# Full-attention layers: exponentials of one key tile on VectorE instead of ScalarE

## The chip, the cores and the metric

The kernel runs on one core of a Trainium2 chip. Its time is the device time of one execution in microseconds: 2757.82 us, the median of 3 runs (2757.58 to 2761.83).

## What is computed

Four attention layers in turn over a sequence of 2048 rows of 512 values: layer norm, projection to queries, keys and values (32 heads of 16), attention, output projection, addition to the input. Layers 0 and 2 see a window of 256 keys, layers 1 and 3 all 2048. Cut to the full layer:

```python
qkv = (layernorm(x) @ wqkv).reshape(B, S, 3, 32, 16)
scores = einsum("bhqd,bhkd->bhqk", q, k) * 16 ** -0.5
p = softmax(scores)
x = x + einsum("bhqk,bhkd->bhqd", p, v).reshape(B, S, 512) @ wo
```

## The kernel before, in words

**Tiles.** The queries are cut into 4 chunks of 512 rows (`c`), the heads into 8 quads of 4 (`qd`), the keys into 16 tiles of 128 (`j`). In a full layer `attn_full` (L763) walks a quad's 16 key tiles. A tile has two halves `pr` of two heads. For each half `exps` issues 8 score matmuls on TensorE (L727, rows `s<-qt,kt`) into one of two PSUM tiles `s` of 128x1024, and one exponential on ScalarE (L735, `e<-s`), so a quad has 32 of them. The values of a key tile (L779, `acc<-e,vt`) are 8 matmuls that add into the two banks `acc`. They are not issued at once but put into `pvq`, and `flush` issues them a tile later, in front of the next tile's second half. A column of ones in `vt` gives the softmax's denominator.

**The end of a quad.** Behind its last values `epilogue` (L683) adds the two `acc` banks on VectorE into `sa` (L415 and L416) and transposes it into `ot`; the next quad's first values need these banks again. The division by the denominator and, for every second quad, the transpose and split into two fp16 parts `oh` (L709 to L712, the low part on GpSimd) follow from a queue.

**Side work.** All else of the layer and much of the next one is cut into `Work` objects: projections (`project`, `values`), the output projection (`wo`, `wo_part`), layer norm, and checks of the weights' range (`verify`). `Side.share` puts some of their matmuls between the key tiles. In a full layer they use one side bank of two PSUM banks, `PH["halves"]` (rows `b`), which VectorE reads out (`join`, L415 and L416 with `j` or `vt`; L653 and L677 with `x`) before the next use.

**What sets the order.** In the full layers the order on TensorE and VectorE is written by the program itself with a planner's clock: every matmul adds an estimate to `clock`, a key tile takes at least 1.8. VectorE's work that can wait goes into four queues `VQ` (`soon`); `drain` issues it when the estimate `vt_` of VectorE's backlog is less than 0.2 ahead of `clock`. Both engines then work in exactly that order, each waiting where data isn't ready. ScalarE takes the exponentials in the order of their scores. In the windowed layers only TensorE's order is fixed in this way, and a step's exponentials go through GpSimd's masks before the values (L812).

## Time and profile before

| | us |
|---|---|
| median of 3 runs | 2757.82 |
| profiled execution | 2759.5 |
| its span | 2757.7 |
| prologue and layer 0 (0 to 495.2) | 495.2 |
| layer 1, full (495.2 to 1447.0) | 951.8 |
| layer 2, windowed (1447.0 to 1783.6) | 336.6 |
| layer 3, full (1783.6 to 2737.8) | 954.2 |
| tail | 19.9 |

In rows of the profile PE is TensorE, DVE is VectorE, ACT is ScalarE, POOL is GpSimd. A group's row has the line, the engine, the operation, output and input tiles with their shapes, the count, then the busy time in us, the mean duration of one in ns, and the idle time before them with what ended it. A row of the timeline has the start, the time to the end, and the same names. A row of waits has who waited for whom, the total in us, how often, and the longest.

### The profile page before, as it was taken

The page shows a single profiled execution, that of the slowest core. Times are in us where ns is not written, and L with a number is a line of the kernel's source. Part 1 is how long each engine was busy: PE and PEld are TensorE (multiplying, and loading weights), DVE is VectorE, ACT ScalarE, POOL GpSimd, SP SyncE. Part 2 cuts the span into 40 slices and gives each one's busy share as a digit, 9 for nine tenths or more (in the row PEclk, how much of TensorE's full clock was granted, in tenths as well). Part 3 has the DMA queues.
Part 4 walks back from the last instruction along what each step waited for, and adds up shares of the span by engine and source line. Part 5 has one row for each costly group of instructions (what it writes and reads, how often), then busy time and mean ns, then how long its engine had stood idle before and what let it go on. Part 6 is the DMA issues. An engine that isn't in the chain of part 4 may idle for free.

```text
span 2757.7 us, 112292 instructions
## 1 busy us (share of the span) xinstructions
PE 2496.1 (91%) x50513; PEld 1100.3 (40%) x50513; DVE 1094.9 (40%) x2314; ACT 2362.9 (86%) x2683; POOL 515.8 (19%) x1074
## 2 busy tenths in 40 slices
PE   7888989999989999999998898899899999998987
PEld 3233334444433344444443333534444444433332
DVE  5564554122343335325326566323333333333333
ACT  4556654899999999999995667399999999999997
POOL 1445552001000000100105678100000000000000
PEclk9999999999999999999999999999999999999999
DMA  8888856322342224324225565623232333333332
GB/s 286 226 241 240 244 178 191 96 83 82 100 120 79 86 93 137 102 78 126 93 73 169 157 181 143 175 72 109 84 107 90 98 97 104 112 104 123 114 120 103
DMA packets 335035, 359.67 MB, mean 130 GB/s; under 512 B 113616, under 2 KB 250320, under 8 KB 328144
## 3 DMA queue, kind: packets, MB, share of 16 engines
q1 hardware_dynamic: 334544, 352.40, 42.3%
q8 instruction: 397, 6.50, 1.0%
q14 instruction: 94, 0.77, 0.1%
HBM read 239.60 MB, written 96.99 MB: 122 GB/s over the span
## 4 chain that ended last, share of the span: by engine, by line
ACT 56%; PE 23%; issue 11%; DVE 5%; DMA 3%; POOL 2%; SPq 0%; ACTq 0%; DVEq 0%; POOLq 0%
ACT e L735 55%; PE b L402 10%; PE acc L812 3%; PE acc L779 3%; PE bs L402 2%; PE s L731 2%; PE s L727 2%; PE b L399 1%; POOL e L802 1%; POOL e L805 1%; DMA qt<-qs 1%; DMA kt<-kw 0%; DMA wr<-in_A_wo_dram 0%; DVE ot L694 0%; DMA w<-wd 0%
## 5 line engine op out<-in xcount | busy, mean ns | idle before, releaser
L735 ACT ACTIVATE e<-s 128x1024 f32<-128x1024 f32 (+2 forms) x2432 | 2238.8, 1058 | 121.0 <-PE s L731 95.3
L779 PE MATMUL acc<-e,vt 64*17 64x512 f32 x16384 | 1085.0, 590 | 1.3 <-issue 1.3
L727 PE MATMUL s<-qt,kt 64*32 64x512 f16 x16384 | 849.0, 380 | 130.4 <-ACT e L735 106.6
L727 PEld LDWEIGHTS <-kt 64*32 64x32 f16 x16384 | 406.7, 89 | 944.2 <-issue 868.8
L779 PEld LDWEIGHTS acc<-e,vt 64*17 64x17 f32 x16384 | 280.5, 92 | 61.1 <-issue 1.5
L805 POOL TENSOR_SCALAR_AFFINE_SELECT e<-e 128x256 f32<-128x256 f32 x512 | 224.9, 446 | 196.5 <-ACT e L735 195.4
L802 POOL TENSOR_SCALAR_AFFINE_SELECT e<-e 128x256 f32<-128x256 f32 x448 | 198.1, 449 | 114.1 <-ACT e L735 112.3
L712 POOL TENSOR_TENSOR oh<-o,oh 128x512 f16<-128x512 f32 x31 | 36.1, 1165 | 938.1 <-DVE oh L711 884.8
L812 PE MATMUL acc<-e,vt 128*17 128x384 f32 (+2 forms) x2816 | 204.7, 396 | 5.3 <-POOL e L802 4.0
L731 PE MATMUL s<-qt,kt 64*128 64x384 f16 (+2 forms) x1408 | 129.0, 280 | 64.0 <-ACT e L735 38.2
L415 DVE TENSOR_SCALAR sa<-acc 128x512 f32<-128x512 f32 x64 | 44.3, 692 | 335.4 <-PE acc L779 335.4
L402 PE MATMUL b<-xc,w 128*128 128x512 f16 x696 | 166.1, 390 | 7.0 <-DMA w<-wd 5.8
L677 DVE SCALAR_TENSOR_TENSOR x<-b,x 128x512 f32<-128x512 f32 x122 | 83.9, 688 | 193.0 <-PE b L399 189.8
L402 PEld LDWEIGHTS <-w 128*128 128x128 f16 x816 | 77.4, 100 | 122.8 <-issue 35.8
L521 POOL TENSOR_TENSOR sq<-sp 128x512 bf16<-128x512 f16 x28 | 41.0, 1463 | 442.2 <-DVE sp L515 427.6
L506 ACT ACTIVATE sp<-b 128x512 f16<-128x512 f32 x58 | 34.7, 598 | 103.3 <-PE b L402 91.2
L731 PEld LDWEIGHTS <-kt 64*128 64x128 f16 x1408 | 54.4, 94 | 167.6 <-issue 137.0
L521 POOL TENSOR_TENSOR sq_h<-sp_h 128x512 bf16<-128x512 f16 x27 | 40.1, 1484 | 409.8 <-DVE sp_h L515 409.8
L399 PE MATMUL b<-wo,oh 64*32 64x512 f16 x2592 | 109.9, 376 | 6.2 <-DVE x L677 3.1
L399 PE MATMUL b<-xc,w 64*32 64x512 f16 x2688 | 110.9, 376 | 3.0 <-DVE j L416 2.3
L399 PE MATMUL b<-xc,w_h 64*32 64x512 f16 x2592 | 104.4, 376 | 4.1 <-DVE km L562 3.9
L415 DVE TENSOR_SCALAR j_h<-b 128x512 f32<-128x512 f32 x27 | 18.7, 691 | 218.7 <-PE b L399 187.6
(136 smaller groups left out, 1874.8 us busy)
## 6 DMA issues: line engine op xcount, KB each, us to landing
kt<-kf SPq DMA_DIRECT2D x128, 512.0 KB
qt<-qs SPq DMA_DIRECT2D x128, 256.0 KB
xd<-x SPq DMA_DIRECT2D x96, 256.0 KB
x<-xd SPq DMA_DIRECT2D x96, 256.0 KB
w<-wd SPq DMA_DIRECT2D x22, 1024.0 KB
kt<-kw SPq DMA_DIRECT2D x64, 256.0 KB
qs<-sp SPq DMA_DIRECT2D x48, 256.0 KB
wo<-wd SPq DMA_DIRECT2D x12, 1024.0 KB
```

What stands on the lines that cost most here:

```text
L399: nc.tensor.matmul(ps[g:g + 32, r], a[k, g:g + 32], b[k], start=(i == 0), stop=(i == len(pairs) - 1), skip_group_check=True)
L402: nc.tensor.matmul(ps, a, b, start=(i == 0), stop=(i == len(pairs) - 1))
L415: nc.vector.tensor_scalar(dst, ps[0], scale, None, op0=ALU.mult)
L521: nc.gpsimd.tensor_tensor(sq, sp[:, 0], sp[:, 0], ALU.mult)
L677: nc.vector.scalar_tensor_tensor(xs[i], p, 1 / WS, xs[i], op0=ALU.mult, op1=ALU.add)
L727: nc.tensor.matmul(ps[g:g + 32, h], kt[R * h:R * h + R, pr, kc + g:kc + g + 32], qt[R * h:R * h + R, pr], start=True, stop=True, skip_grou ...
L731: nc.tensor.matmul(ps[:, h, s0:s0 + wd_], kt[R * h:R * h + R, pr, kc:kc + P], qt[R * h:R * h + R, pr, qc:qc + wd_], start=True, stop=True)
L735: nc.scalar.activation(e[:, :, w0:w1], ps[:, :, w0:w1], AF.Exp, scale=SCALE)
L779: nc.tensor.matmul(acc[r][32 * h:32 * h + DH + 1, :], V[l, qd // 4, j // 8][k, j % 8, 4 * (qd % 4) + h, :], es_[h // 2][k, h % 2, :], star ...
L802: nc.gpsimd.affine_select(v, v, pattern=[[0, 2], [-1, P]], compare_op=ALU.is_gt, fill=0.0, base=0, channel_multiplier=1)
L805: nc.gpsimd.affine_select(v, v, pattern=[[0, 2], [1, P]], compare_op=ALU.is_ge, fill=0.0, base=0, channel_multiplier=-1)
L812: nc.tensor.matmul(a[32 * h:32 * h + DH + 1, q * P:(q + nb) * P], V[l, (4 * c + j) // 4][:, j % 4, 4 * qd + h, :], es_[h // 2][:, h % 2, s ...
```

## The change

One key tile of each quad, `DJ` = 7, is taken out of `attn_full`'s walk. Its two halves (`unit`) are scored into the side bank when that is free, and VectorE computes the exponential: one instruction reads the bank, scales and clamps the scores and writes them as integers in the layout of a float's bits; then for each head of the half two bitwise instructions split exponent and mantissa, and four SCALAR_TENSOR_TENSOR evaluate a polynomial. They stand in a queue of their own, `VQ[3]`. The values of this tile (`unit_values`) are issued when the planner takes them for ready, and at the latest in front of the quad's last values. A factor `LEAD` of the polynomial is put into this tile's values, so that a half that stays on ScalarE gets a bias `lead`. `units` decides: not when the planner's estimate of VectorE's backlog with 8.5 more would pass the quad's end. The next quad's tile may begin in this one.

```diff
-EB, XB, XNB, WB, VB, OB = 6, 4, 4, 2, 3, 5
+EB, XB, XNB, WB, VB, OB = 5, 4, 4, 2, 3, 5
+DJ = 7
+AHEAD = 0.7
...
     def drain(upto=None):
...
-        while vt_[0] <= clock[0] + 0.2:
-            q = next((q for q in VQ if q), None)
+        while vt_[0] <= clock[0] + AHEAD:
+            order = VQ[:2] + VQ[3:4] if PH["mid"] else VQ if not UX or UX[0]["quad"] == PH["quad"] else VQ[:3] + VQ[4:] + VQ[3:4]
+            q = next((q for q in order if q and (q[0][2] is None or q[0][2]())), None)
...
     def epilogue(l, c, qd, a):
...
-            (nc.gpsimd if l % 2 and (l, c, qd) != (3, NQ - 1, NQD - 1) else nc.vector).tensor_tensor(hl[:, 1], o, hl[:, 0], ALU.subtract)
+            nc.vector.tensor_tensor(hl[:, 1], o, hl[:, 0], ALU.subtract)
...
+    def unit(u):
+
+        pr = len(u["e"])
+        n = u["n"] + f"_{pr}"
+        ps = PH["halves"]
+        for g in range(0, P, 32):
+            for h in range(2):
+                nc.tensor.matmul(ps[g:g + 32, h], u["kt"][R * h:R * h + R, pr, DJ % 8 * P + g:DJ % 8 * P + g + 32],
+                                 u["qt"][R * h:R * h + R, pr], start=True, stop=True, skip_group_check=True)
+        spent(0.27)
+        PH["free"] = clock[0] + 1.5
+        t = pp.tile([P, 2, QC], I32, name=f"d{n}", tag="d", bufs=2)
+        vec(1.2)
+        nc.vector.tensor_scalar(t, ps, SCALE * LOG2E * 2.0 ** 23, -2.0 ** 30, op0=ALU.mult, op1=ALU.max)
+        u["e"].append(t.bitcast(F32))
+        u["left"] += 2
+        for h in range(2):
+            x, m, p = t[:, h], [], []
+
+            def a(h=h, x=x, m=m, p=p):
+                m.append(vp.tile([P, QC], I32, name=f"dm{n}_{h}", tag="oe", bufs=3))
+                nc.vector.tensor_scalar(m[0], x, 0x7FFFFF, 0x3F800000, op0=ALU.bitwise_and, op1=ALU.bitwise_or)
+                nc.vector.tensor_scalar(x, x, 0x3F800000, None, op0=ALU.bitwise_and)
+
+            def b(h=h, m=m, p=p):
+                p.append(vp.tile([P, QC], F32, name=f"dp{n}_{h}", tag="xn", bufs=1))
+                PH["mid"] = True
+                f = m[0].bitcast(F32)
+                nc.vector.scalar_tensor_tensor(p[0], f, POLY[3], f, op0=ALU.add, op1=ALU.mult)
+                nc.vector.scalar_tensor_tensor(p[0], p[0], POLY[2], f, op0=ALU.add, op1=ALU.mult)
+
+            def c(x=x, m=m, p=p):
+                nc.vector.scalar_tensor_tensor(p[0], p[0], POLY[1], m[0].bitcast(F32), op0=ALU.add, op1=ALU.mult)
+                nc.vector.scalar_tensor_tensor(x.bitcast(F32), p[0], POLY[0], x.bitcast(F32), op0=ALU.add, op1=ALU.mult)
+                u["left"] -= 1
+                PH["mid"] = False
+                u["at"] = vt_[0] + 0.4
+            for us, f in ((0.92, a), (1.2, b), (1.2, c)):
+                soon(3, us, f)
+
+    def units():
+
+        u = UX[0]
+        if u["shut"] or len(u["e"]) == 2 or clock[0] < u["ready"]:
+            return False
+        if u["quad"] == PH["quad"]:
+            queued = sum(us for q in VQ[:4] for us, _, _ in q)
+            if max(vt_[0], clock[0]) + queued + 8.5 > PH["end"]:
+                return False
+        if not PH["busy"] and clock[0] >= PH["free"]:
+            unit(u)
+        return True
...
+    def unit_values(l, c, qd, force=False):
+
+        u = UX[0]
+        if u["quad"] != (l, c, qd) or u["shut"]:
+            return False
+        if force:
+            drain(4)
+        elif len(u["e"]) < 2 or u["left"] or clock[0] < u["at"]:
+            return False
+        UX.popleft()
+        values_of(l, qd, DJ, u["e"], False, False)
+        return True
...
     def attn_full(l, c, qd, kt, qt, a):
-        for j in range(NT):
+        js = [j for j in range(NT) if j != DJ]
+        own = [None]
+        for j in js + [DJ]:
...
             def pv(j=j, es_=es_):
+                if j == js[-1] and not own[0] and UX and UX[0]["quad"] == (l, c, qd):
+                    unit_values(l, c, qd, True)
...
     def side2(c):
         if c == 0:
-            return [OO(1, 3), Q(2, 2), T(2, 3), K(2, 3)]
+            return [OO(1, 3), Q(2, 2), VV(2, 2), T(2, 3), K(2, 3)]
...
-            a += [OO(1, c), T(2, c)] + ([Q(2, c - 1, False)] if c else []) + [K(2, c, False), VV(2, c, False)]
+            a += [OO(1, c), T(2, c)] + ([Q(2, c - 1, False)] if c else []) + [K(2, c, False)] + ([VV(2, c, False)] if c < 2 else [])
```

Along with it: `EB`, the buffers of `e`, falls from 6 to 5 to make room; the planner's estimates of a score tile and of a tile's values in a full layer fall from 0.27 and 1.0 to 0.23 and 0.88, and `Side.share` allows up to 2.5 instead of 1.5 side steps at once; `Side` counts 15 steps a quad; `verify` works in pieces of 128 columns through a fifth queue, which may run into the next layer; the low part of `oh` is computed on VectorE in the full layers too; one of layer 2's value projections moves from layer 1's side work into layer 2's first chunk.

Where it shows on VectorE: around the drain of `acc` at the end of quad 5 of chunk 1 in layer 3. Names end in layer, chunk, quad; `d` is the polynomial's tile, `dm` its mantissa, `dp` the polynomial, `sa` the drain, `x` an addition to the input, `km` a maximum. Before:

```order
L575 TENSOR_SCALAR m3_2_2_46716<-b3_33034 32x512
L576 SCALAR_TENSOR_TENSOR m3_2_2_46716<-b3_33034,m3_2_2_46716 32x512
L677 SCALAR_TENSOR_TENSOR x3_4_45967<-b3_33034,x3_4_45967 128x512 x2
L562 TENSOR_REDUCE km3_30693<-b3_33034 32x1
L677 SCALAR_TENSOR_TENSOR x3_5_45969<-b3_33034,x3_5_45969 128x512 x2
L677 SCALAR_TENSOR_TENSOR x3_6_45971<-b3_33034,x3_6_45971 128x512 x2
L415 TENSOR_SCALAR sa3_1_5_47185<-acc0_81 128x512
L416 SCALAR_TENSOR_TENSOR sa3_1_5_47185<-acc1_82,sa3_1_5_47185 128x512
L694 STREAM_TRANSPOSE ot3_1_5_47184<-sa3_1_5_47185 128x512
```

And in the changed kernel at the same drain:

```order
L581 TENSOR_REDUCE km3_31324<-b3_33668 32x1
L797 SCALAR_TENSOR_TENSOR dp3_1_5_1_0_48108<-dp3_1_5_1_0_48108,dm3_1_5_1_0_48075 128x512
L798 SCALAR_TENSOR_TENSOR d3_1_5_1_47820<-dp3_1_5_1_0_48108,d3_1_5_1_47820 128x512
L786 TENSOR_SCALAR dm3_1_5_1_1_48188<-d3_1_5_1_47820 128x512
L787 TENSOR_SCALAR d3_1_5_1_47820<-d3_1_5_1_47820 128x512
L793 SCALAR_TENSOR_TENSOR dp3_1_5_1_1_48191<-dm3_1_5_1_1_48188 128x512
L794 SCALAR_TENSOR_TENSOR dp3_1_5_1_1_48191<-dp3_1_5_1_1_48191,dm3_1_5_1_1_48188 128x512
L797 SCALAR_TENSOR_TENSOR dp3_1_5_1_1_48191<-dp3_1_5_1_1_48191,dm3_1_5_1_1_48188 128x512
L798 SCALAR_TENSOR_TENSOR d3_1_5_1_47820<-dp3_1_5_1_1_48191,d3_1_5_1_47820 128x512
L432 TENSOR_SCALAR sa3_1_5_48213<-acc0_81 128x512
L433 SCALAR_TENSOR_TENSOR sa3_1_5_48213<-acc1_82,sa3_1_5_48213 128x512
L720 STREAM_TRANSPOSE ot3_1_5_48212<-sa3_1_5_48213 128x512
```

The drain stood behind additions that TensorE had fed earlier; now it stands behind the last instructions of the quad's own polynomial tile.

On TensorE at the same place, between the next quad's second score tile and its third (`acc<-e..15` are the last values of the quad, `acc<-d` those of the polynomial tile). Before:

```order
L727 MATMUL s3_2_4_0_1_47165<-qt3_2_4_47134,kt3_2_4_0_47136 32x512
L779 MATMUL acc0_81<-e3_1_5_15_0_47102,vt3_1_1_39531 17x512
L779 MATMUL acc1_82<-e3_1_5_15_0_47102,vt3_1_1_39531 17x512
L779 MATMUL acc0_81<-e3_1_5_15_0_47102,vt3_1_1_39531 17x512
L779 MATMUL acc1_82<-e3_1_5_15_0_47102,vt3_1_1_39531 17x512
L779 MATMUL acc0_81<-e3_1_5_15_1_47121,vt3_1_1_39531 17x512
```

And changed:

```order
L754 MATMUL s3_2_4_0_1_48177<-qt3_2_4_48146,kt3_2_4_0_48148 32x512
L827 MATMUL acc0_81<-d3_1_5_0_47777,vt3_1_0_33603 17x512
L827 MATMUL acc1_82<-d3_1_5_0_47777,vt3_1_0_33603 17x512
L827 MATMUL acc0_81<-d3_1_5_0_47777,vt3_1_0_33603 17x512
L827 MATMUL acc1_82<-d3_1_5_0_47777,vt3_1_0_33603 17x512
L827 MATMUL acc0_81<-d3_1_5_1_47820,vt3_1_0_33603 17x512
L827 MATMUL acc1_82<-d3_1_5_1_47820,vt3_1_0_33603 17x512
L827 MATMUL acc0_81<-d3_1_5_1_47820,vt3_1_0_33603 17x512
L827 MATMUL acc1_82<-d3_1_5_1_47820,vt3_1_0_33603 17x512
L827 MATMUL acc0_81<-e3_1_5_15_0_48123,vt3_1_1_40450 17x512
```

The polynomial tile's 8 value matmuls stand in front of the quad's last ones, and the next quad's remaining scores behind both.

More of the change, by code (lines that the diff above doesn't have):

```diff
@@ L659, in wo @@
             yield -MM if PH["full"] else -12 * MM
+        OFREE.update((l, c, t) for t in range(NHT))
         if PH["full"]:
@@ new lines, in values_of @@
+    def values_of(l, qd, j, es, first, last):
+        for h in range(4):
+            for r in range(2):
+                k = slice(R * r, R * r + R)
+                nc.tensor.matmul(acc[r][32 * h:32 * h + DH + 1, :], V[l, qd // 4, j // 8][k, j % 8, 4 * (qd % 4) + h, :],
+                                 es[h // 2][k, h % 2, :], start=first, stop=last, skip_group_check=True)
+    def unit_values(l, c, qd, force=False):
[9 more added lines that the diff above has]
+        return True
```

159 lines of the change are left out of this document (103 added, 56 removed).

## The prediction

> **What bounds the kernel now.** I read the page's first part, then the table of stretches, cut where the rows of `e` on ScalarE begin and end each layer, then ScalarE's groups and TensorE's waits inside the full layers. A quad is written (layer, chunk, quad), as in the tile names.
>
> ```profile
> span 2757.7 us, 112292 instructions
> PE 2496.1 (91%) x50513; PEld 1100.3 (40%) x50513; DVE 1094.9 (40%) x2314; ACT 2362.9 (86%) x2683; POOL 515.8 (19%) x1074
> ```
>
> ```profile
> core 0: us, PE busy (x) PEld busy (x) DVE busy (x) ACT busy (x) POOL busy (x), PEclk, DMA share, GB/s
> 495.20:1447.00 951.80, 888.19 (x22576) 400.74 (x22559) 320.24 (x640) 944.12 (x1026) 59.46 (x46) 1.00 0.31 94
> 1447.00:1783.60 336.60, 298.71 (x2893) 129.92 (x2886) 195.80 (x455) 202.18 (x255) 198.91 (x483) 0.98 0.58 167
> 1783.60:2737.80 954.20, 869.18 (x21558) 385.22 (x21550) 306.65 (x576) 943.94 (x1024) 57.52 (x42) 1.00 0.33 102
> ```
>
> The second and fourth stretches are the full layers, 1906.0 of 2757.7 us. ScalarE is busy in 99% of both (944.12 of 951.80, 943.94 of 954.20), VectorE in a third. ScalarE's group in layer 1, and whom TensorE waits for there:
>
> ```profile
> L735 ACT ACTIVATE e<-s 128x1024 f32<-128x1024 f32 x1024 | 943.8, 1074 | 7.7 <-PE s L727 7.1
> ```
>
> ```profile
> PE s L727 <- ACT e L735: 43.7, 119, 1.1
> PE b L399 <- DVE j L416: 3.0, 4, 0.8
> ```
>
> So exponentials follow each other without a gap: 943.8/1024 = 0.922 us each (the 1074 ns overlap), 29.5 us for a quad's 32. TensorE waits for them, and for VectorE almost never. TensorE has little to spare itself; in this piece of layer 1 the starts leave no hole:
>
> ```profile
> 998.71 1.05 PE L779 MATMUL acc<-e,vt 64*17 64x512 f32 x16
> 999.56 0.41 PE L727 MATMUL s<-qt,kt 64*32 64x512 f16 x8
> 999.78 0.63 PE L399 MATMUL b<-wo,oh 64*32 64x512 f16 x16
> 1000.33 0.41 PE L727 MATMUL s<-qt,kt 64*32 64x512 f16 x8
> 1000.54 1.05 PE L779 MATMUL acc<-e,vt 64*17 64x512 f32 x16
> ```
>
> Values take 0.85 us to the next start (1.05 to their end), a score tile 0.22, two side steps 0.55: 1.83 us a step, beside ScalarE's 1.84.
>
> **What goes.** The new order has 111 of the 128 tiles on VectorE (53 in layer 1, 58 in layer 3); the other 17 stay on ScalarE with a bias. That takes 111 x 0.922 = **102.3 us** off ScalarE, and 47 quads have 30 tiles left (27.7 us), 17 have 31 (28.6 us). TensorE's matmuls are the same ones in other places.
>
> **What VectorE gets.** Prices come from these groups and from the starts in a run of its instructions.
>
> ```profile
> L416 DVE SCALAR_TENSOR_TENSOR sa<-acc,sa 128x512 f32<-128x512 f32 x64 | 44.3, 692 | 6.6
> L515 DVE CAST sp<-j 128x512 f16<-128x512 f32 x28 | 12.0, 427 | 1.8
> L562 DVE TENSOR_REDUCE km<-b 128x1 f32<-128x1024 f32 x3 | 3.7, 1225 | 5.0 <-PE b L543 5.0
> L712 DVE TENSOR_TENSOR oh<-o,oh 128x512 f16<-128x512 f32 x33 | 23.8, 720 | 0.8
> ```
>
> ```profile
> 1288.08 0.69 DVE L448 TENSOR_TENSOR xh<-xn,xh 128x512 f16<-128x512 f32 x1
> 1288.80 0.55 DVE L442 TENSOR_SCALAR xn<-x,mv,y 128x512 f32<-128x512 f32 x1
> 1289.27 0.54 DVE L442 TENSOR_SCALAR xh<-x,mv,y 128x512 f16<-128x512 f32 x1
> ...
> 1293.37 0.69 DVE L448 TENSOR_TENSOR xh<-xn,xh 128x512 f16<-128x512 f32 x1
> 1293.98 1.10 DVE L350 TENSOR_REDUCE wa<-wc 128x128 f32<-128x512 f32 x1
> 1295.30 0.69 DVE L415 TENSOR_SCALAR j<-b 128x512 f32<-128x512 f32 x1 [0.22 <-PE b L399]
> 1296.03 0.69 DVE L416 SCALAR_TENSOR_TENSOR j<-b,j 128x512 f32<-128x512 f32 x1
> 1296.76 0.43 DVE L515 CAST sp<-j 128x512 f16<-128x512 f32 x1
> ```
>
> An instruction that needs the one in front (`j` after `j`, or `xn` over a tile still being read) starts 0.73 us after a 0.69 us one, its duration and 0.035; one that doesn't starts 0.61 after it, its duration less 0.08. A polynomial tile is one read of 128x1024 from the side bank (as `km`: 1.22, so 1.14 to the next), and for each of two halves two bitwise instructions and a chain of four SCALAR_TENSOR_TENSOR: 0.61 + 3 x 0.73 = 2.8. No large bitwise integer instruction is in the trace. Its bounds are the CAST (0.43) and the 0.69 of everything that runs at full length. I take 0.43, the nearest as an instruction with one tensor from SBUF, so a half costs about 0.8 + 2.8 = 3.6 and a tile 1.14 + 7.2 = **8.4 us**, against 7.84 in the planner. By 0.69 it is 9.4. The Trainium skill, "VectorE: DVE Perf Modes", section "The perf-mode tier table", gives fp32 `tensor_scalar` in SBUF double rate and anything two-sourced single rate; the CAST and SCALAR_TENSOR_TENSOR rows agree, and by it the 0.43 would stand, though no row here shows it for integers.
>
> 111 tiles make 932 us; 31 low parts that GpSimd computed add 31 x 0.7 = 22. VectorE's load becomes about 320 + 53 x 8.4 + 16 x 0.7 = 776 of ScalarE's 971 x 0.922 = 895 us in layer 1, and 307 + 58 x 8.4 + 15 x 0.7 = 805 of 966 x 0.922 = 891 in layer 3. On average it fits. Quad by quad it does not. Between the drains of `acc` of (3,1,4) and (3,1,5) there now stand:
> - two polynomial tiles, 16.8 us
> - the drain, scaling and transposes of the quad before, 4.2
> - one join and split of a projection, 2.5
> - two additions to `x` 2.7, one `m` 1.3, one `km` 1.1
>
> The small terms are each row's duration by the rule above; together 27.7 us (with rounding). And as the order shows, in 38 quads the last polynomial instruction stands right before the drain, and TensorE's values of that tile right before the quad's last ones. TensorE can't start them before VectorE is done, VectorE can't drain before they end: 0.85 + 1.05 = 1.9 us in which VectorE has nothing. The quad lasts 27.7 + 1.9 = 29.6 on this loop, 2.0 more than ScalarE's 27.7, and behind the waiting values stand the next quad's scores, so ScalarE runs dry.
>
> The same sum over the 62 other quads (31 in each layer; the first of each left out) gives VectorE 762 and 785 us beside ScalarE's 866 and 863. What exceeds ScalarE quad by quad is 47.7 us in layer 1 (12.0 in (1,2,4), where a layer norm falls in; 9.9 in (1,3,4), 7.1 in (1,3,7)) and 38.9 in layer 3 (18 quads with 0.6 to 3.5, two with 0.1, and (3,3,7) with 7.3): **+86.6 us**. A quad with room to spare doesn't pay for it, since each drain starts anew from TensorE. Bounds: without the 1.9 us it is 43; with 0.69 for the bitwise instructions, 166.
>
> **Smaller terms.**
> - Inside a quad VectorE also waits for TensorE to fill the side bank: in (3,1,5) its first tile's scores stand behind the sixth step's. I can't sum that from rows; 0 to 30, I take +10.
> - Layer 1 now ends with 25 side steps behind its last score (200 matmuls; before, no gap had more than 4 steps), and TensorE has to put the same side work into shorter quads: 0 to 20, I take +4, since most of it lies beside (1,3,7)'s excess.
> - One value projection goes from layer 1 to layer 2: 48 matmuls.
>
> ```profile
> L402 PE MATMUL b<-xc,w 128*128 128x512 f16 x96 | 23.9, 405 | 0.0
> L812 PE MATMUL acc<-e,vt 128*17 128x384 f32 (+2 forms) x2816 | 204.7, 396 | 5.3 <-POOL e L802 4.0 <-DVE ot L694 0.8 <-POOL e L805 0.2
> ```
>
>   At 23.9/96 they cost 12 us on TensorE, busy 89% of that layer: 3 to 12, I take +10. In layer 1 ScalarE hid them.
> - Five `e` buffers where six were: in the windowed layers the second exponential of a step must wait for the values of two steps earlier, which TensorE issues behind that step's scores (1.07 us a step: 204.7/192), where it now waits 0.92 for the first. Behind it on ScalarE stand evictions of projections. 0 to 0.2 us in 192 steps, 0 to 38; I take +4, as ScalarE is busy only 202 of 337 us there.
> - Seven of the weight checks move into layer 2, where VectorE idles 141 us (nothing); SP's and GpSimd's queues lose or keep what they had.
>
> **The sum.** 2759.5 (the profiled execution) - 102.3 + 86.6 + 10 + 4 + 10 + 4 = 2771.8. The median of the runs shown is 1.7 lower: **2770**. The gain on ScalarE is real; I expect VectorE's loop at the quads' ends to take it back.
>
> **Rivals.**
> 1. **VectorE's tiles come in time** (faster). If instructions follow 0.61 apart also where I price 0.73, or the values are ready ahead, only the load itself counts: 43 in place of 96.6, so 2770 - 54 = 2716. For it: 38 drains depend on a loop whose slack I priced from four rows. Against it: `j` after `j` is 0.73 wherever they follow. It decides below some 7.7 us a tile.
> 2. **The bitwise instructions run at full length**: 166 in place of 86.6, 2850. Then VectorE holds both layers.
> 3. **The windowed layers pay for the fifth buffer**: 38 in place of 4, 2804. It decides where a step has less than about 1 us of side work to cover it; TensorE waited for ScalarE only 23.5 us in layer 2, which speaks against it:
>
> ```profile
> PE s L731 <- ACT e L735: 23.5, 43, 1.1
> ```
>
> That the change doesn't do what it says is excluded by the count of 111.
>
> **How the numbers follow.** A run can tell about 0.2% from no change: 5.5 us. Forecast 0.50, with its own range 2740 to 2805 (waits 0 to 30, the loop 70 to 110): of it 0.05 faster, 0.10 same, 0.35 slower. Rival 1 0.30, rival 2 0.13, rival 3 0.07. Faster 0.35, same 0.10, slower 0.55. The range runs from 2705, below rival 1, to 2835; rival 2's upper part and a change that costs nothing are left out.
>
> **What would show it.** ScalarE's idle time in the two full layers, 18 us now, should grow to some 120, put down to TensorE's scores; TensorE should show waits for VectorE's `d` at the values, 1 to 4 us each and one near 12 in (1,2,4); `sa` should wait about 2 us for `acc` where `d` stood in front. VectorE should be busy 80 to 86% of these layers and ScalarE 92 to 95%. The bitwise rows settle 0.43 or 0.69. Layer 2 should be 337 + 10 to 15 us. If TensorE hardly waits for `d`, rival 1 holds and the step with the loop was wrong.

## The result, and the profile after

The changed kernel takes 2881.34 us (median of 4 runs, 2880.14 to 2883.96) beside 2759.05 (4 runs, 2757.58 to 2761.83): 1.0443 times as long, 95% interval 1.0425 to 1.0461. Of all the runs below one, of e2 (3001.48 us), was in a slower state of the chip and is left out. The profiled execution took 2883.96 us. First the head of its page and its chain of work:

```profile
span 2882.2 us, 112925 instructions
PE 2526.1 (88%) x50177; PEld 1098.3 (38%) x50177; DVE 2021.3 (70%) x3882; ACT 2292.2 (80%) x2576; POOL 479.3 (17%) x1047
...
ACT 34%; PE 31%; DVE 21%; issue 8%; DMA 4%; POOL 1%; SPq 1%; ACTq 0%; DVEq 0%; POOLq 0%
```

No engine is saturated any more, not even in the full layers (ScalarE 92 and 90%, TensorE 91 and 89%). The same table of stretches as before; the third one is new, a gap behind layer 1's last exponential:

```profile
core 0: us, PE busy (x) PEld busy (x) DVE busy (x) ACT busy (x) POOL busy (x), PEclk, DMA share, GB/s
0.00:504.10 504.10, 433.87 (x3448) 182.15 (x3449) 264.38 (x621) 277.81 (x381) 200.40 (x505) 0.96 0.77 226
504.10:1481.70 977.60, 886.03 (x21944) 390.50 (x21936) 741.33 (x1363) 903.64 (x972) 37.32 (x28) 0.98 0.28 86
1481.70:1499.50 17.80, 11.66 (x252) 4.23 (x251) 10.06 (x17) 0.00 (x0) 5.05 (x6) 0.90 0.45 155
1499.50:1864.20 364.70, 302.28 (x2923) 132.82 (x2922) 205.94 (x511) 210.61 (x259) 196.76 (x482) 0.99 0.55 163
1864.20:2862.50 998.30, 885.32 (x21574) 386.73 (x21581) 791.57 (x1350) 900.11 (x966) 39.72 (x27) 0.98 0.31 98
2862.50:2882.20 19.70, 6.92 (x54) 1.92 (x38) 8.06 (x23) 0.00 (x0) 0.00 (x0) 0.76 0.38 125
```

Beside before: layer 0 +8.9, layer 1 +25.8 and its gap +17.8, layer 2 +28.1, layer 3 +44.1 (14.6 of it behind its last exponential), the rest -0.2: +124.5, the difference of the spans. The exponentials went as planned (971 and 966 of 1024), and ScalarE's busy time in the two full layers fell by 84.3 us (944.12 + 943.94 before, 903.64 + 900.11 now). Both layers are longer all the same. ScalarE's groups in layer 1 and, in the second fence, in layer 3:

```profile
L762 ACT ACTIVATE e<-s 128x1024 f32<-128x1024 f32 x960 | 893.2, 1061 | 73.9 <-PE s L754 70.4 <-ACT e L762 0.3
L762 ACT ACTIVATE e<-s,lead 128x1024 f32<-128x1024 f32 x11 | 12.8, 1160 | 0.0
```

```profile
L762 ACT ACTIVATE e<-s 128x1024 f32<-128x1024 f32 x960 | 895.0, 1053 | 83.8 <-PE s L754 80.2
```

Idle time before exponentials is 73.9 + 83.8 = **157.7 us**, where it was 7.7 + 11.1 = 18.8, nearly all of it put down to TensorE's scores. This sum, "ScalarE's idle time" below, is what the experiments follow. Whom TensorE waits for in layer 1:

```profile
PE s L754 <- ACT e L762: 35.9, 96, 1.1
...
PE acc L827 <- DVE sa L432: 21.6, 4, 6.2
...
PE acc L827 <- DVE d L798: 9.3, 6, 4.9
```

Four waits for the drain `sa` hold 21.6 us; before there was none worth a row. In layer 3 the waits for `d` are:

```profile
PE acc L827 <- DVE d L798: 11.2, 7, 2.5
```

A "tile on VectorE" is from here on one half of a key tile, one 128x1024 exponential; a quad has at most two. VectorE's groups:

```profile
L778 DVE TENSOR_SCALAR d<-b 128x1024 int32<-128x1024 f32 x111 | 135.4, 1220 | 77.9 <-PE b L772 77.9
L786 DVE TENSOR_SCALAR dm<-d 128x512 int32<-128x512 int32 x222 | 98.3, 443 | 1.3
L787 DVE TENSOR_SCALAR d<-d 128x512 int32<-128x512 int32 x222 | 94.9, 427 | 7.6
L793 DVE SCALAR_TENSOR_TENSOR dp<-dm 128x512 f32<-128x512 f32 x222 | 154.4, 695 | 0.2
```

The bitwise instructions take 0.44 and 0.43, the others what was read from before.

Now a quad's end that looks harmless, (1,0,2): TensorE, then ScalarE.

```profile
588.50 0.41 PE L754 MATMUL s<-qt,kt 64*32 64x512 f16 x8
588.71 1.05 PE L827 MATMUL acc<-e,vt 64*17 64x512 f32 x16
589.57 0.41 PE L754 MATMUL s<-qt,kt 64*32 64x512 f16 x8
589.78 1.05 PE L827 MATMUL acc<-d,vt 64*17 64x512 f32 x16
590.64 1.05 PE L827 MATMUL acc<-e,vt 64*17 64x512 f32 x16
591.50 0.41 PE L754 MATMUL s<-qt,kt 64*32 64x512 f16 x8
```

```profile
587.36 3.83 ACT L762 ACTIVATE e<-s 128x1024 f32<-128x1024 f32 x4
592.04 1.02 ACT L762 ACTIVATE e<-s 128x1024 f32<-128x1024 f32 x1 [0.85 <-PE s L754]
```

TensorE has no hole here and waits for nobody. But between two score tiles stand two groups of values, so the scores start 1.93 us apart (589.57 to 591.50), and there are just two `s` tiles. At best a score starts when the exponential two before it ends, and its own exponential follows 0.54 us behind that start (591.50 to 592.04). So two tiles cover a slot of some 2 x 0.92 - 0.54 = 1.3 us between two starts (an estimate from these rows), not 1.93. ScalarE idles 0.85 at the next quad's third exponential. 32 quads have 0.6 to 3 us there, 40.2 together; in some of them VectorE adds to it.

In the second kind of idle time TensorE waits for the polynomial tile itself. At the end of (3,2,3), TensorE, VectorE and ScalarE:

```profile
2481.81 0.61 PE L827 MATMUL acc<-d,vt 64*17 64x512 f32 x2 [2.54 <-DVE d L798]
```

```profile
2483.74 0.69 DVE L432 TENSOR_SCALAR sa<-acc 128x512 f32<-128x512 f32 x1 [1.98 <-PE acc L827]
```

```profile
2484.02 2.85 ACT L762 ACTIVATE e<-s 128x1024 f32<-128x1024 f32 x3 [5.01 <-PE s L754]
```

This is the loop of the prediction: TensorE waits 2.54 for `d`, then VectorE 1.98 for the values, and the third exponential of (3,2,4) comes 5.01 late. Five quads of layer 3 have such a stall of 3 to 5.4 us, and the longest of all, 15.83 in front of the third exponential of (1,2,5), begins in the same way (TensorE waits 4.93 for `d`).

The third kind is at the sixth exponential, here 7.13 us in (1,1,5): VectorE, then ScalarE.

```profile
880.88 1.22 DVE L778 TENSOR_SCALAR d<-b 128x1024 int32<-128x1024 f32 x1 [2.01 <-PE b L772]
...
888.69 0.69 DVE L798 SCALAR_TENSOR_TENSOR d<-dp,d 128x512 f32<-128x512 f32 x1
889.30 0.68 DVE L432 TENSOR_SCALAR sa<-acc 128x512 f32<-128x512 f32 x1
```

```profile
893.29 3.11 ACT L762 ACTIVATE e<-s 128x1024 f32<-128x1024 f32 x3 [7.13 <-PE s L754]
```

The order has a whole tile of quad (1,1,5) in front of the drain of quad (1,1,4): `drain(4)`, called for the last half of (1,1,4)'s own tile, empties the queue of all that waits there. VectorE spends 8.4 us on it (880.88 to 889.30) before it drains the accumulator, and TensorE's next values, with the scores behind them, wait. Five quads have this, 36.3 us together.

### The profile page after: what moved, and what is told of

The parts are those of the page before. It is cut to its first block, busy times and chain, and to the rows that moved or that the text cites. A ratio compares the mean times of both kernels' runs of the same rounds, so it can differ in the third digit from the quotient of the medians.

```text
span 2882.2 us, 112925 instructions
## 1 busy us (share of the span) xinstructions
PE 2526.1 (88%) x50177; PEld 1098.3 (38%) x50177; DVE 2021.3 (70%) x3882; ACT 2292.2 (80%) x2576; POOL 479.3 (17%) x1047
## 4 chain that ended last, share of the span: by engine, by line
ACT 34%; PE 31%; DVE 21%; issue 8%; DMA 4%; POOL 1%; SPq 1%; ACTq 0%; DVEq 0%; POOLq 0%
ACT e L762 33%; PE b L419 9%; PE acc L827 8%; PE acc L929 4%; PE s L754 3%; PE b L416 2%; DVE d L778 2%; PE s L758 2%; PE bs L419 2%; DVE x L701 2%; DVE dp L797 2%; DVE dp L794 1%; DVE dp L793 1%; DVE d L798 1%; DVE d L787 1%
## 5 line engine op out<-in xcount | busy, mean ns | idle before, releaser
L762 ACT ACTIVATE e<-s 128x1024 f32<-128x1024 f32 (+2 forms) x2304 | 2150.2, 1043 | 315.7 <-PE s L754 150.5
L827 PE MATMUL acc<-e,vt 64*17 64x512 f32 x15496 | 1069.1, 596 | 26.8 <-DVE sa L432 26.8
L754 PE MATMUL s<-qt,kt 64*32 64x512 f16 x15496 | 827.9, 382 | 112.4 <-ACT e L762 88.8
L754 PEld LDWEIGHTS <-kt 64*32 64x32 f16 x15496 | 374.7, 90 | 837.6 <-issue 764.4
L827 PEld LDWEIGHTS acc<-e,vt 64*17 64x17 f32 x15496 | 271.8, 93 | 117.5 <-DVE sa L432 28.3
L778 DVE TENSOR_SCALAR d<-b 128x1024 int32<-128x1024 f32 x111 | 135.4, 1220 | 77.9 <-PE b L772 77.9
L797 DVE SCALAR_TENSOR_TENSOR dp<-dp,dm 128x512 f32<-128x512 f32 x222 | 158.4, 714 | 6.6
L794 DVE SCALAR_TENSOR_TENSOR dp<-dp,dm 128x512 f32<-128x512 f32 x222 | 154.5, 696 | 7.7
L798 DVE SCALAR_TENSOR_TENSOR d<-dp,d 128x512 f32<-128x512 f32 x222 | 153.6, 692 | 7.5
L793 DVE SCALAR_TENSOR_TENSOR dp<-dm 128x512 f32<-128x512 f32 x222 | 154.4, 695 | 0.2
L432 DVE TENSOR_SCALAR sa<-acc 128x512 f32<-128x512 f32 x64 | 44.2, 690 | 132.1 <-PE acc L827 131.9
L720 DVE STREAM_TRANSPOSE ot<-acc 128x512 f32<-128x512 f32 x64 | 45.6, 712 | 119.3 <-PE acc L929 119.1
```

Of the source, the lines that this page charges most:

```text
L754: nc.tensor.matmul(ps[g:g + 32, h], kt[R * h:R * h + R, pr, kc + g:kc + g + 32], qt[R * h:R * h + R, pr], start=True, stop=True, skip_grou ...
L762: nc.scalar.activation(e[:, :, w0:w1], ps[:, :, w0:w1], AF.Exp, scale=SCALE, **bias)
L778: nc.vector.tensor_scalar(t, ps, SCALE * LOG2E * 2.0 ** 23, -2.0 ** 30, op0=ALU.mult, op1=ALU.max)
L793: nc.vector.scalar_tensor_tensor(p[0], f, POLY[3], f, op0=ALU.add, op1=ALU.mult)
L794: nc.vector.scalar_tensor_tensor(p[0], p[0], POLY[2], f, op0=ALU.add, op1=ALU.mult)
L797: nc.vector.scalar_tensor_tensor(p[0], p[0], POLY[1], m[0].bitcast(F32), op0=ALU.add, op1=ALU.mult)
```

## The experiments

All ratios are to the kernel before, run beside on the same chip (medians 2756.57 to 2758.82 us); the changed kernel has 1.0443. "Idle" is ScalarE's idle time before exponentials in both full layers; before it is 18.8, after 157.7. Some expectations count it by wider measures (173 or 181 us where this one has 157.7, 95 where it has 73.4), so only the steps between kernels compare. What leaves a part of the work out says so: e2 and e12 to e18.

| run | median us | ratio, 95% interval | idle us |
|---|---|---|---|
| e1 no tiles | 2802.04 | 1.0156 (1.0132 to 1.0179) | 19.8 |
| e2 short chain | 2825.24 | 1.0229 (1.0197 to 1.0260) | 103.3 |
| e3 five e | 2791.30 | 1.0114 (1.0088 to 1.0139) | 20.6 |
| e4 values moved | 2765.58 | 1.0022 (1.0011 to 1.0033) | 16.3 |
| e5 own first | 2878.03 | 1.0431 (1.0413 to 1.0448) | 140.7 |
| e6 own, split | 2859.15 | 1.0363 (1.0341 to 1.0384) | 132.1 |
| e7 seven in windows | 2859.26 | 1.0363 (1.0346 to 1.0380) | 156.5 |
| e8 all three | 2828.80 | 1.0259 (1.0242 to 1.0277) | 129.0 |
| e9 two groups | 2804.06 | 1.0150 (1.0132 to 1.0169) | 60.8 |
| e10 one tile | 2801.03 | 1.0151 (1.0135 to 1.0166) | 81.8 |
| e11 true costs | 2926.42 | 1.0604 (1.0589 to 1.0618) | 193.5 |
| e12 read only | 2799.29 | 1.0157 (1.0140 to 1.0174) | 73.4 |
| e13 free, apart | 2797.18 | 1.0141 (1.0124 to 1.0158) | 106.1 |
| e14 free, one | 2776.56 | 1.0067 (1.0050 to 1.0083) | 65.5 |
| e15 thin before | 2754.22 | 0.9982 (0.9972 to 0.9991) | 13.4 |
| e16 thin after | 2874.58 | 1.0423 (1.0405 to 1.0442) | 154.7 |
| e17 thin, read only | 2790.32 | 1.0112 (1.0093 to 1.0131) | 73.2 |
| e18 in turn | 2828.77 | 1.0260 (1.0244 to 1.0277) | 85.9 |

### What lies outside the full layers: e1, e3, e4, e7

The change with no tile on VectorE:

```diff
     def units():
+        return False
```

> The changed kernel with no polynomial tile at all: all 32 exponential tiles of a quad stay on ScalarE (tile 7 last, with its bias), everything else is as changed: five e buffers, the value projection moved to layer 2, the order of the side work. If what the tiles do on VectorE and TensorE makes the whole loss in the full layers, those two layers are as long as before the change (951.8 and 954.2 us, ScalarE idle 20 us in both), the gap at layer 1's end is gone, and only layers 0 and 2 are longer, by the 9 and 28 us of the changed kernel: 2759 + 37 = 2796. If layer 2's loss comes from side work that the tiles pushed there, layer 2 falls back to about 337 + 10 and the time is about 2778. If the new order of the side work itself costs the full layers something, the time is above 2800.

2802: the first case. ScalarE idles 19.8 us, and no work is left behind layer 1; the full layers are 957 and 960 us. What the change does there comes from the tiles themselves; its other parts cost 43 us, some 11 of them in the full layers. Two of them alone in the kernel before:

```diff
-EB, XB, XNB, WB, VB, OB = 6, 4, 4, 2, 3, 5
+EB, XB, XNB, WB, VB, OB = 5, 4, 4, 2, 3, 5
```

> The kernel before with five e buffers in place of six, nothing else. The prediction had +4 us over layers 0 and 2: 2763. If the waits of the exponentials for the values of two steps earlier are what layers 0 and 2 lost (49 waits of 1.0 us in the middle in layer 2 after the change), it is +9 in layer 0 and +10 to 17 in layer 2: 2778 to 2785. The full layers keep their time in both.

2791, +32 and above both cases. Layer 0 is 8.9 us longer (504.4 beside 495.5, to the first exponential of layer 1), layer 2 17.3 (352.4 beside 335.1, exponential to exponential), the full layers some 4 together. In layer 2 of this kernel exponentials now wait for values two steps earlier, a row that before doesn't have:

```profile
ACT e L735 <- PE acc L812: 26.1, 50, 1.7
```

> The kernel before with the value projection of layer 2's third column block done in layer 2 in place of layer 1, nothing else. The prediction had +10 us (its 48 matmuls at 0.25 us are 12 us on TensorE, busy 89% of that layer): 2769. If such a step hides in TensorE's gaps it is +3: 2762. If it also pushes the steps behind it, whose results layer 3 waits for, it is over +15: 2775 and more.

The edit is the last two pairs of lines of the diff. +7; layer 2 is 5.3 longer. The fifth buffer is the larger part by far. The opposite test gives the windowed layers of the changed kernel the two idle `d` buffers:

```diff
-        e = pp.tile([P, 2, QC], F32, name=f"e{name}", tag="e", bufs=EB)
+        PH["en"] = (PH.get("en", 0) + 1) % 7
+        if PH["full"] or PH["en"] < 5:
+            e = pp.tile([P, 2, QC], F32, name=f"e{name}", tag="e", bufs=EB)
+        else:
+            e = pp.tile([P, 2, QC], F32, name=f"e{name}", tag="d", bufs=2)
```

> The changed kernel, but in the windowed layers the exponentials also use the two d buffers, which lie idle there: seven buffers in place of five. If the fifth buffer alone made layers 0 and 2 longer (26 us in the run with five buffers in the kernel before), they fall to about 495 and 355 us, and the time to 2881 - 26 = 2855. If the moved value projection or the left-over side work makes layer 2 longer, only layer 0's 9 us go: 2872.

-22: layer 0 falls from 504.2 to 497.9, layer 2 from 364.0 to 345.9, the idle time in the full layers stays. The row of waits is gone there. So the fifth buffer cost 22 to 26 us in the windowed layers.

### VectorE taken away: e2, e12

First about half of a tile is left out (e2), then all but the read of its scores (e12), TensorE's order untouched. The edit of e2, cut to the first two of the four instructions:

```diff
-                nc.vector.scalar_tensor_tensor(p[0], f, POLY[3], f, op0=ALU.add, op1=ALU.mult)
+                z = slice(0, 64)
+                nc.vector.scalar_tensor_tensor(p[0][:, z], f[:, z], POLY[3], f[:, z], op0=ALU.add, op1=ALU.mult)
...
```

> The changed kernel with the same instructions in the same order, but the four SCALAR_TENSOR_TENSOR of each half work on 64 of 512 columns (the polynomial is left out for the other 448, whose values are the bits of the exponent alone). A VectorE tile falls from 8.4 to about 4 us, so VectorE can no longer be late at a quad's end. By the prediction's step (VectorE's loop at the quad's end) ScalarE's idle time in the full layers falls from 173 to about 30 us and the time to about 2881 - 143 = 2738. If the idle time comes from TensorE's order (the tile's values stand directly before the last values, with the next quad's scores behind both), some 0.8 to 1 us of each of 64 quads stays: about 2881 - 110 = 2770 to 2800. The gap at layer 1's end (18 us) and layers 0 and 2 (37 us) stay in both.

2825, above both cases: idle falls only from 157.7 to 103.3. The stalls of 3 us and more fall from 12 (78.4 us) to 6 (29.9); the 0.8 us at third exponentials stay (38 quads have 0.6 to 3 us).

> The changed kernel with TensorE's instructions word for word in the same order, but of a polynomial tile VectorE does only the read of the scores (1.2 us; it writes ones, and the exponential of these tiles is left out). VectorE can be late for nothing. What idle time of ScalarE is left in the full layers (181 us with the whole tile, 126 with half of it, 23 in the kernel before) is TensorE's own order. If that order sets it, 90 to 110 us stay: the full layers are within 10 us of the kernel before and the time is 2800 to 2820. If VectorE's load is still what half a tile left, it falls to 25 to 40 and the time to about 2735.

2799, the first case, but the full layers are 21 and 9 us shorter than before (930.8 and 945.4 between first and last exponential). ScalarE in its layer 1:

```profile
L762 ACT ACTIVATE e<-s 128x1024 f32<-128x1024 f32 x960 | 892.1, 1062 | 28.2 <-PE s L754 24.7 <-ACT e L762 0.3
```

With 45.2 in layer 3 that is 73.4: VectorE's polynomial is worth **84.3 us** of idle time, and 54.6 above the kernel before are there without it. (That it is also the busy time ScalarE was spared is chance.) Third exponentials have 33.7 us here and 79.3 in the changed kernel, sixth ones 7.7 and 39.6: so 45.6 of the 84.3 us stand where the prediction's loop acts, 31.9 where a tile is in front of the drain. The 45.6 are in 22 quads; the third exponentials of the other 42 are alike in both kernels to 0.1 us. Of the long stalls one is left (5.5). (1,0,2) lasts 28.50 us in both kernels, and its stall is the same:

```profile
591.01 2.86 ACT L762 ACTIVATE e<-s 128x1024 f32<-128x1024 f32 x3 [0.84 <-PE s L754]
```

### TensorE's order, or TensorE's room: e9, e15 to e18

> The kernel before, with no VectorE tile; only the values of a quad's tile 14 are issued one slot later, directly in front of those of tile 15 (between the next quad's second and third scores). No work is added. If TensorE can't issue two groups of values (2 x 0.85 us) between two scores without ScalarE running dry, each of 63 quads gets 0.5 to 0.85 us of idle time at its third exponential: 32 to 54 us more, 2790 to 2813. If the idle time of the changed kernel comes from VectorE alone, nothing changes: 2759 within 6.

The edit in the kernel before is one condition:

```diff
                         if f is None:
-                            flush(1)
+                            if u:
+                                flush(1)
```

2804, the first case. ScalarE in layers 1 and 3 waits 28.5 and 32.3 us, 62 quads have 0.6 us or more at their third exponential, 42.6 us together, and the rest is as before. TensorE, then ScalarE at (3,2,7):

```profile
2693.34 1.91 PE L779 MATMUL acc<-e,vt 64*17 64x512 f32 x32
2695.05 0.62 PE L727 MATMUL s<-qt,kt 64*32 64x512 f16 x14
```

```profile
2691.07 3.83 ACT L735 ACTIVATE e<-s 128x1024 f32<-128x1024 f32 x4
2695.59 1.94 ACT L735 ACTIVATE e<-s 128x1024 f32<-128x1024 f32 x2 [0.69 <-PE s L727]
```

Two groups of values between two scores cost 0.7 us a quad without any VectorE tile. In e12 third exponentials hold 33.7 us of the 54.6; 37 quads have 0.6 us or more, and in 36 of them both groups, `acc<-d` and `acc<-e`, stand between the second score and the third. For the rest I took TensorE's lack of room, and cut its side work in the full layers to an eighth of the columns between a group's first and last matmuls, in three kernels:

```diff
-                        nc.tensor.matmul(ps[g:g + 32, r], a[k, g:g + 32], b[k], start=(i == 0), stop=(i == len(pairs) - 1),
+                        n = b.shape[-1] // (8 if 0 < i < len(pairs) - 1 else 1)
+                        nc.tensor.matmul(ps[g:g + 32, r, :n], a[k, g:g + 32], b[k, :n], start=(i == 0), stop=(i == len(pairs) - 1),
```

> The kernel before, with the same instructions in the same order, but in the full layers the side projections' matmuls between the first and the last of a group work on an eighth of their columns (the rest of those products is left out). It is the control: ScalarE is saturated there, idle 23 us in two layers. If that holds, nothing changes but those 23 us: 2740 to 2759.

> The changed kernel with the same cut of the side projections: TensorE has some 250 us less to do in the two full layers. If TensorE's lack of room is what costs the 72 us of idle time that stayed with VectorE taken away, and the steps left over at the ends of layers 1 and 3 (30 us), some 40 of the 72 go (the two groups of values side by side stay, 34) and 10 of the 30: about 2881 - 50 = 2830. If VectorE's load alone sets the pace, nothing changes: over 2865.

> Both taken away: VectorE only reads the scores of its tiles, and TensorE has the cut side projections; TensorE's order is still word for word that of the changed kernel. ScalarE's idle time in the full layers was 95 us with VectorE alone taken away. If TensorE's room is the rest, about 55 are left (34 of them the two groups of values at the third exponential, which stay): 2799 - 40 - 10 = 2750. If the rest is in the order itself, 85 to 95 are left and the time is 2780 or more.

The control behaves (2754), and the theory falls: 2875 and 2790, idle 154.7 and 73.2 where it was 157.7 and 73.4. The room was made, though less than the expectation says: TensorE is busy 1604 us in e17's full layers and 1722 in e12's, 118 less and not 250. In layer 1 of e17 TensorE waits for ScalarE 104.3 us, in e12 35.9; ScalarE's own wait stays as it was (24.2 beside 24.7):

```profile
PE s L755 <- ACT e L763: 104.3, 296, 1.1
ACT e L763 <- PE s L755: 24.2, 32, 5.4
```

So it is not how much TensorE has to do. For 33.7 us it is where the groups stand; the other 21 are spread over small gaps whose cause wasn't found. The last run moves only that, in e12:

```diff
                         if f is None:
+                            if u == 0 and UX and PH.get("two"):
+                                unit_values(*PH["two"], True)
                             flush(1)
...
+                            PH["two"] = None
+                            if u == NT - 2 and UX and UX[0]["quad"] == (l, c, qd) and not UX[0]["shut"]:
+                                PH["two"] = (l, c, qd)
+                                flush(1)
+                                sd.lag += 0.85
                             sd.step()
```

> The kernel in which VectorE only reads the scores of its tiles, and at a quad's end the groups of values stand one by one between scores (tile 14 behind the quad's last score, the VectorE tile behind the next quad's first, tile 15 behind its second) in place of tile 14 alone and then the VectorE tile and tile 15 together. No work is added or taken. If the two groups together are what idles ScalarE at the third exponential (34 us in 47 quads there), most of it goes: 20 to 34 us below 2799, at 2765 to 2779. Four slots of 1.07 us in a row against tiles of 0.92 may keep some 0.1 to 0.4 us of each quad. If the idle time only moves to another score, it stays within 8 us of 2799.

The stalls at third exponentials are gone (33.7 to 11.8 us, 1 quad in place of 37 with 0.6 to 3), as the first case has it, but the time rose to 2829, outside both cases. First exponentials gain 16.1 us (8.3 to 24.4), about 0.25 a quad, as the expectation allowed. The order shifts as well: two new stalls of 7 and 11 us, one that grows from 5.5 to 11, and 30.6 us between layer 1's last exponential and layer 2's first (15.9 in e12). So the cause of the stalls at third exponentials is shown; that the idle time goes away with them is not.

### Versions: e5, e6, e8, e10, e11, e13, e14

```diff
         if force:
-            drain(4)
+            while u["left"]:
+                give(VQ[3])
...
                 if j == DJ:
-                    drain(4)
+                    while own[0]["left"]:
+                        give(VQ[3])
```

> The changed kernel, but where a quad's values need its polynomial tile, only the rest of that tile is put in front on VectorE, not all that waits there (in the changed kernel a whole tile of the next quad goes along, and stands before the drain of acc). The order has 108 tiles on VectorE in place of 111, and 104 matmuls behind layer 1's last score in place of 208. If the stalls of 6 to 8 us at the sixth exponential of a quad (five quads, 36 us together) come from the drain behind the next quad's tile, they go: 2881 - 36 + 3 - 8 = 2840, and TensorE's waits for sa (21.6 us in layer 1, 5.2 in layer 3) go with them. If they come from VectorE's load by itself (the prediction's loop), the tile only moves and the time stays above 2865.

The five stalls at the sixth exponential (36.3 us) are gone, with the four waits for `sa`; (1,1,5) falls from 35.4 to 27.9 us. But the time fell by only 3, which fits the second case: in (1,1,5), (1,2,6) and (3,0,5) the stall is gone, in (1,3,1) and (1,3,5) it stands at the third exponential instead (7.3 and 9.5 us), (1,3,7) gets a new one of 6.3, and the gap behind layer 1 grows from 17.9 to 34.2. The place in front of the drain was the cause in three of the five quads; in the other two VectorE is late all the same. With the tile's values in two halves, each when its half is ready:

> As the last kernel, and the values of a quad's two polynomial tiles are issued tile by tile, the first one's as soon as VectorE has finished it, the second one's at the latest before the last values. TensorE then has 0.43 us in one step in place of 0.85 directly before the last 0.85. If the 0.8 us that ScalarE idles at the third exponential of most quads (46 us in 63 quads that the shorter polynomial left in place) come from two groups of values back to back on a TensorE without slack, half or more of them goes: 25 to 45 us below the last kernel, about 2805. If they come from VectorE finishing late, the time is that of the last kernel within 10 us.

> The three edits together: own tile first, values tile by tile, seven buffers in the windowed layers. If the three causes are separate, the time is that of the second kernel of this job less 26: about 2780. Then what is left over 2759 is the gap at layer 1's end (about 18 us) and the moved projection (7), and ScalarE's 100 us of saved tiles are still mostly eaten in the full layers. If the causes overlap, it stays above 2795.

19 us below e5, less than forecast: 27 quads still have 0.6 to 3 us at the third exponential, as the second tile's values stand beside the last ones there (in most of them 8 matmuls `acc<-d` with the 16 of `acc<-e`). e8 adds e7's edit, for another -30, and stays in its second case. Then at most one tile a quad (`len(u["e"]) == 1` in `units`), and separately a planner with the tile's measured price:

> The three edits of the last job (own tile first, values tile by tile, seven buffers in the windowed layers) and at most one VectorE tile in a quad: 64 tiles in place of 108, so VectorE's load between two drains of acc is about 19 of 28.5 us and nothing is left over at layer 1's end. ScalarE is spared 64 x 0.92 = 59 us; layers 0 and 2 cost about 12. If a tile in the middle of a quad, with its values in a slot of its own, costs ScalarE nothing, the time is 2759 - 59 + 12 = 2712; with some 0.5 us of idle time left in each quad it is 2744. If every tile costs what it brings, 2765 to 2775. It is a version that may beat both kernels.

> The three edits, with the planner's costs of a tile as measured (a half 0.86 + 1.4 + 1.4 in place of 0.92 + 1.2 + 1.2, VectorE's queue planned 0.2 us ahead in place of 0.7), its gate at 10.5 us before a quad's end in place of 8.5, and the last tile's values at the latest in the slot before the next quad's first score, not beside the last values. 95 tiles in place of 108. If the planner's 7.84 us for a tile of 8.4 are why VectorE is late at the drains, the stalls of over 3 us go (some 70 us in the three-edit version) and with them the gap at layer 1's end (8 matmuls left in place of 216): 2829 + 13 x 0.92 - 70 - 17 = 2754. If the two groups of values and TensorE's fullness are the limit, about 2790 to 2800.

One tile a quad saves 59 us and costs 63 of idle time, here in many small gaps; 2801 is above every case. e11 also changes what is computed (which step does it wasn't found), so only its waits are read: third exponentials fall to 19.5 us, but the values, due one slot earlier, wait for VectorE, and 21 quads' first exponentials come 3 to 9 us late. For the bound of what tiles can bring, e8 and e10 with only the read on VectorE:

> The three-edit version, again with only the read of the scores on VectorE (ones in place of the exponential), and the planner told so: all 128 tiles go there, each tile's values stand in a slot of their own inside the quad, none beside the last values. It is the bound of what the tiles can bring. ScalarE has 960 tiles of 0.92 in a layer: 883 us. If the place of the values was the limit, the exponentials of a full layer take 895 to 910 us. If TensorE's fullness (888 us busy of 951 in layer 1 before) is the limit, layer 1 takes 930 us or more and layer 3, where less side work is left, less than that. What it leaves over at layer 1's end is not counted.

> The one-tile version (64 tiles, 972 us in each full layer with the whole polynomial), again with only the read of the scores on VectorE. ScalarE has 992 tiles: 912 us a layer. If the polynomial's load was what cost the 60 us of idle time a layer there, the exponentials of a layer take 920 to 930. If it is TensorE's order around a quad's end (31 tiles, the half of tile 7 that stays on ScalarE last), they stay at 950 or more.

Layer 1's exponentials take 950.7 and 959.0 us, layer 3's 958.2 and 969.0, so in these two orders even tiles that cost VectorE 1.2 us don't make the layers shorter than 951.5 and 954.2 by more than 1 us. In e12's order they do, by 29.5 in both together; there the windowed layers and the layers' ends take more than that back. In e13 side work falls behind and is forced out in blocks of up to 208 matmuls between two scores. e14 is left with small gaps I can't put to one cause. No version of the change beat the kernel before.

## Why the prediction was wrong

The direction was forecast; the time lies 46 us above the range. Term by term, in us:

| term | predicted | measured |
|---|---|---|
| ScalarE's saved exponentials | -102.3 | -84.3 of busy time |
| VectorE in the full layers (loop 86.6, waits 10) | +96.6 | +84.3 (157.7 less e12's 73.4) |
| TensorE's side work in shorter quads, layer 1's end | +4 | +54.6 (e12's 73.4 less 18.8), +30.8 at both layers' ends (16.4 and 14.4) |
| value projection moved | +10 | +5.3 (e4) |
| fifth buffer | +4 | +26.2 (e3: 8.9 + 17.3) |
| sum | +12.3 | +116.9 of 124.5 |

Some 6 of the missing 8 are in layer 2, beyond e3 and e4 added.

- **The failed step** is the one on TensorE: "TensorE has to put the same side work into shorter quads: 0 to 20, I take +4". I had printed TensorE's two groups of values side by side and asked only what VectorE waits for there (1.9 us), not what waits for TensorE. It took TensorE's cost as a question of load, where the runs show the order of its groups: a second group makes a slot 1.93 us, two score tiles cover some 1.3, and e9 prices that at 0.7 us a quad (33.7 of the 54.6 us in e12). e17 shows that it isn't load. What holds the other 21 us stays open.
- **The ends of the layers** belong to that step. Layer 1's left-over steps don't lie beside (1,3,7)'s excess as I had it: the program finishes them before the quad's last values, one at a time through the one side bank, so that each waits for VectorE's join. Layer 3's end has six such groups of matmuls where it had two (34.3 us from the last exponential to the end, 19.9 before). TensorE behind layer 1's last exponentials:

```profile
1482.88 2.78 PE L416 MATMUL b<-xc,w 64*32 64x512 f16 x96 [2.32 <-DVE j L433]
1487.21 2.78 PE L416 MATMUL b<-xc,w 64*32 64x512 f16 x96 [1.54 <-DVE j L433]
1491.53 0.40 PE L562 MATMUL b<-sq,hsum 64*32 64x512 bf16 x6 [1.54 <-DVE j L433]
1493.66 0.39 PE L562 MATMUL b<-sq,hsum 64*32 64x512 bf16 x2 [1.73 <-POOL sq L540]
1493.67 1.51 PE L827 MATMUL acc<-e,vt 64*17 64x512 f32 x16
```

- **The fifth buffer** was rival 3, at 38 in place of 4 and with a chance of 0.07. The row I held against it counted TensorE's waits for ScalarE; what decides is ScalarE's wait for TensorE's values, which the trace of before could not show, as six buffers hid it. Its size was nearer the bound than the value I took.
- **VectorE's term** has nearly the right size, in part by luck. The price of a tile holds (8.4 us, bitwise at 0.43 and 0.44, so rival 2 is out; what the prediction drew from the Trainium skill, "VectorE: DVE Perf Modes", section "The perf-mode tier table", holds for integers in these rows too). The loop at the quads' ends is real, with its wait of 1.98 us for 1.9, but it costs 45.6 us and not 86.6: 15 in the one place foreseen, behind (1,2,4), with a layer norm and a check in the queue (a stall of 15.8 where 12.0 was written), and 30.6 in 21 other quads, 24.7 of them in layer 3. In most quads it costs nothing; (1,0,2) is as long without VectorE. Another 31.9 come from five quads where the next quad's tile stands before the drain, whose lateness a sum of the work between drains does not see. The two together come near the forecast by chance. (The example's terms add up to 28.6 us, not 27.7.) The wait for the side bank, taken as 10, can't be told apart in these runs.
- **ScalarE's term** lost 18: busy time is 0.93 an exponential in place of 0.922 (893.2/960). One with a gap behind it counts its full 1.04 us, where the next one else starts after 0.917. By the trace 219 stand behind a gap in the full layers, 44 before, so some 175 x 0.12 = 21 us (an estimate) would explain it; no run tried it.
- **The signs**: idle time 158 for 120, VectorE busy 76 and 79% (80 to 86 expected), ScalarE 92 and 90% (92 to 95), layer 2 365 (347 to 352). TensorE waits for `d` 9.3 and 11.2 us, 13 times and up to 4.9, where waits of 1 to 4 and one near 12 were expected. That fits a loop that acts in a third of the quads; the prediction named "hardly waits" as the sign that it is wrong.
- **The range** took each unknown's bound alone. Even with all of them at their upper ends (loop 110, waits 30, TensorE 20, projection 12, buffer 38) its sum would have been 2866, still below 2881: TensorE's term lies outside its own bounds, 85 us where 20 was the most.

## What to carry to other kernels

When work is taken from the engine that sets the pace, look at every slot between two of its inputs: if the feeder's longest slot exceeds what the buffers between them cover (here 1.3 us with two tiles of 0.92), the engine idles there, even if the feeder has room on average. A buffer given up for the change may be paid in another stage, here the windowed layers. And price an instruction put in front of a drain by the drain's lateness, not by the sum of work between drains.

## What the runs showed of the hardware

TensorE's clock fell without a long pause. At layer 3's end groups of 24 matmuls alternate with waits of 1.54 us for VectorE's additions; from the fourth on they take 1.48 us where they took 0.84, and the granted clock reads 0.96 and then 0.50. The third row of the second fence is the end of layer 1, with groups of 96 and the same waits of 1.54:

```profile
2851.23 0.84 PE L416 MATMUL b<-wo,oh 64*32 64x512 f16 x24 [1.54 <-DVE x L701]
2853.61 1.48 PE L416 MATMUL b<-wo,oh 64*32 64x512 f16 x24 [1.54 <-DVE x L701]
```

```profile
2846.00:2853.60 7.60, 3.00 (x94) 1.31 (x80) 4.62 (x7) 1.88 (x3) 0.00 (x0) 0.96 0.58 174
2853.60:2861.00 7.40, 4.32 (x80) 1.62 (x87) 2.77 (x4) 0.00 (x0) 0.00 (x0) 0.50 0.47 145
1480.00:1494.00 14.00, 6.87 (x232) 3.49 (x224) 8.88 (x15) 1.62 (x2) 4.44 (x3) 1.00 0.47 161
```

The Trainium skill, "TensorE: Matmul & The Clock Gate", section "A second HAM failure mode: psum-queue depth-cycling", says that a TensorE which pauses briefly and often between groups can lose its full clock. The trace agrees: after 3.00 us busy in 7.60 (39%) the clock fell, with 6.87 in 14.00 (49%) it stayed at 1.00.
